# W2's conversion moves from the stage after the attention into the planned order of the attention

## The chip, the cores and the metric

The program runs on one core of a Trainium2 chip. The metric is the time of one execution on the device in microseconds (us). The engines have these names in the profile: PE is TensorE's matmuls and PEld its weight loads, DVE is VectorE, ACT is ScalarE, POOL is GpSimd and SP is SyncE, which here issues every transfer. Each engine works off its own list of instructions in order and waits where a semaphore tells it to.

## The reference

The input goes through a windowed attention (4 sequences of 576 positions, 8 heads of 64) and two blocks of dense layers. Weights that arrive as 64-bit floats are marked with a star.

```python
attn = softmax(mask(q @ k.T / 8))            # each position sees itself and the 63 before it
x    = (attn @ v) as [4, 576, 512]
h    = relu(x @ w_in)                         # w_in* [512, 1024]
u, v = halves of h;  v = layer_norm(v)
x    = (u * (w_spatial @ v + b)) @ w_out      # w_out* [512, 512]
u    = x + (relu(x.T @ w_tok1) @ w_tok2).T    # w_tok1*, w_tok2*
out  = u + relu(u @ w_ch1) @ w_ch2            # w_ch1* [512, 1536] (W1), w_ch2* [1536, 512] (W2)
```

## The kernel before

Every matrix product is done three times on fp32r operands: each operand is split into a high half (a cast on ACT) and a low half (value minus high half, a subtraction on DVE or POOL), and high x high, high x low and low x high are added up in one PSUM bank.

A weight that arrives as 64-bit words is first made into 32-bit floats. ACT scales the upper word (`down`, L136), DVE shifts the result left (L125) and joins three bits of the lower word to it (L131). In the following text these steps together are called decoding.

The two channel products use Strassen's scheme with seven products. For this, W1 and W2 are each cut into six blocks (j = 0 to 5). For each block of W2 four quarters are decoded, four sums of quarters are formed on POOL (L781), and the eight results are split and stored in the DRAM tile `scr` as pairs of halves, from where the second channel product loads them (`w<-scr`) 63 times.

**The attention stage** (up to about 208 us) is put in order by a planner in the program, the class `Steps`. Every piece of work is a step with an engine, a rank, an estimated time, the steps that it comes after, and buffers that it takes and gives back. The planner plays the stage through with these estimates: at each point it takes, on the engine that is free first, the ready step of the lowest rank, and writes its instructions there. What it writes is the order of each engine. In it the steps of a tile of attention are: scores S (PE), maxima M (DVE), exponentials X (ACT), norm N (DVE, L314 to L316), transposes T (PE, L485), copy C (ACT), product V (PE). Between them PE gets products of the first dense layer (`u`, `v`) and the spatial product (`s`) to fill its time.

**The stage after it** (about 240 to 360 us) holds the product with W_out (`W`, L830), transposes (`T`, L841), the token products (`A`, L849, with the relu `hh` on ACT at L855 and its low half `hl` on DVE at L856; `tok2`, L860) and then the first channel product (L927). Conversions of weights run beside these in slots: an object `bg` of the class `Line` is told after each product how much time it took, and for each 1.25 us it lets each open generator go one step on. A table names the slot at which each block of W1 and W2 begins: before, W2's blocks begin at slots 21, 33, 45, 56, 66 and 106, W1's at 27, 39, 51, 62, 71 and 90. All their instructions stand between those of the products on ACT, DVE and POOL. Names in the rows: `k` are decoded weights, `hl` from L775 and L776 the halves of W2 (another tile than `hl` from L856), `gh` and `gl` the halves of the gated input of W_out, `sh` and `sl` the halves of W1's sums.

**The last stage** (about 360 to 628 us) holds both channel products of three column groups.

## Time and profile before

| what | us |
|---|---|
| median of 3 runs (629.91 to 631.49) | 631.07 |
| the profiled execution | 629.98 |
| its span, first to last instruction | 628.2 |
| PE busy | 603.8 (96%) |
| PEld busy | 562.2 (89%) |
| DVE busy | 464.6 (74%) |
| ACT busy | 348.0 (55%) |
| POOL busy | 152.1 (24%) |

PE is the engine that has work all the time; the end of a matmul is modelled in this profile, so a stretch in which PE is called busy may hide small losses. To see where time can be won or lost, one looks for stretches in which PE is idle and for the instruction that ended the idle time.

### The profile page before, as it was taken

The numbers are of one execution on the slowest core, as the hardware profiler recorded it, in microseconds if no ns is written. First come the engines' busy times: TensorE is split into PE (matmuls) and PEld (weight loads), VectorE is DVE, ScalarE is ACT, GpSimd is POOL, SyncE is SP. The second block draws the span as 40 slices with busy tenths as digits, with TensorE's granted clock in tenths as the row PEclk, the third lists the DMA queues.
The fourth block names the chain that finished last, engine by engine and source line by source line (L and its number), as shares of the span: only waits on it lengthen the run. The fifth ranks groups of instructions, "written<-read, shape, count | busy, mean of one in ns | idle before, by whom it ended". The sixth has DMA issues, their size and how long they took to land.

```text
span 628.2 us, 11904 instructions
## 1 busy us (share of the span) xinstructions
PE 603.8 (96%) x4396; PEld 562.2 (89%) x4396; DVE 464.6 (74%) x980; ACT 348.0 (55%) x849; POOL 152.1 (24%) x169
## 2 busy tenths in 40 slices
PE   4999999999999999999889999999999999999997
PEld 2678899989998998788778898999999999999997
DVE  5999857754475545698878788898975889876882
ACT  5897756653484505686463555546643657444540
POOL 3000200100111000389778317140011140021320
PEclk8899999999999999999989999999999999999999
DMA  8956334440013503368876146674634575434652
GB/s 326 335 181 197 86 110 140 152 143 10 28 42 102 192 1 134 118 218 295 291 267 228 44 165 212 249 259 164 215 127 167 191 241 184 155 136 168 231 197 76
DMA packets 46354, 106.46 MB, mean 169 GB/s; under 512 B 4308, under 2 KB 16856, under 8 KB 46296
## 3 DMA queue, kind: packets, MB, share of 16 engines
q1 hardware_dynamic: 46296, 105.70, 48.8%
q8 instruction: 35, 0.57, 0.4%
q14 instruction: 23, 0.19, 0.1%
HBM read 86.81 MB, written 18.87 MB: 168 GB/s over the span
## 4 chain that ended last, share of the span: by engine, by line
PE 42%; DVE 5%; ACT 2%; issue 1%; ACTq 0%; DVEq 0%
PE A L1139 19%; PE mm L927 10%; PE A L927 8%; PE A L183 3%; DVE sl L171 1%; PE A L1223 1%; PE mm L183 1%; DVE hid L955 1%; DVE room L171 1%; ACT k L136 0%; DVE U L867 0%; DVE hid L921 0%; DVE k L131 0%; PE A L845 0%; ACT hid L952 0%
## 5 line engine op out<-in xcount | busy, mean ns | idle before, releaser
L1139 PE MATMUL A<-room,w 128*128 128x384 f32 x720 | 131.0, 335 | 0.7 <-DVE U L1175 0.7
L1139 PEld LDWEIGHTS A<-room,w 128*128 128x128 f32 x720 | 125.1, 188 | 2.1 <-DVE U L1175 1.0
L1133 ACT CAST room<-hid 128x384 fp32r<-128x384 f32 x120 | 61.3, 513 | 49.6 <-PE A L1139 38.4
L921 POOL TENSOR_TENSOR hid<-hid 128x384 f32<-128x384 f32 x36 | 43.8, 1226 | 181.9 <-DVE hid L921 150.5
L1134 DVE TENSOR_TENSOR room<-hid,room 128x384 fp32r<-128x384 f32 x120 | 73.2, 637 | 13.5 <-ACT room L1133 12.0
L183 PE MATMUL mm<-ws,room 128*128 128x288 f32 x416 | 60.9, 297 | 0.0
L183 PEld LDWEIGHTS mm<-ws,room 128*128 128x128 f32 x416 | 56.7, 188 | 0.5 <-DVE nm L297 0.3
L952 ACT ACTIVATE hid<-hid 128x384 f32<-128x384 f32 x54 | 28.0, 526 | 41.5 <-DVE hid L955 41.4
L776 POOL TENSOR_TENSOR hl<-k,hl 128x512 fp32r<-128x512 f32 (+1 forms) x24 | 31.2, 1305 | 73.8 <-ACT hl L775 72.1
L375 POOL TENSOR_SCALAR rstd<-mv 128x1 f32<-128x1 f32 x18 | 5.3, 296 | 178.8 <-DVE mv L373 165.2
L955 DVE TENSOR_TENSOR hid<-A,hid 128x384 f32<-128x384 f32 x54 | 29.5, 553 | 22.4 <-PE A L927 16.0
L306 ACT ACTIVATE pb<-pb,nm 128x128 f32<-128x128 f32 x96 | 37.2, 392 | 4.8 <-DVE nm L297 4.8
L927 PE MATMUL mm<-room,sh 128*128 128x384 f32 x144 | 37.2, 334 | 0.0
L406 DVE TENSOR_TENSOR U<-mm,U 128x288 f32<-128x288 f32 x32 | 14.6, 457 | 28.6 <-PE mm L183 28.3
L183 PE MATMUL mm<-xh,wi_h 128*128 128x384 f32 x96 | 33.4, 348 | 0.0
L183 PE MATMUL mm<-xh,wi_l 128*128 128x384 f32 x96 | 32.3, 336 | 0.0
L183 PE MATMUL mm<-xl,wi_h 128*128 128x384 f32 x96 | 32.2, 335 | 0.0
L183 PE MATMUL mm<-gh,wo_h 128*128 128x512 f32 (+1 forms) x80 | 30.5, 382 | 1.4 <-DVE U L867 0.9
L183 PE MATMUL mm<-gl,wo_h 128*128 128x512 f32 (+1 forms) x80 | 29.8, 372 | 1.3 <-DVE gl L827 1.3
L183 PE MATMUL mm<-gh,wo_l 128*128 128x512 f32 (+1 forms) x80 | 29.5, 369 | 0.0
L1164 DVE TENSOR_TENSOR U<-A,U 128x384 f32<-128x384 f32 x42 | 21.9, 551 | 10.3 <-PE A L1139 5.7
L485 PE MATMUL sp<-ident,pb 128*128 128x128 f32 x144 | 21.6, 284 | 5.6 <-DVE pb L316 2.1
(175 smaller groups left out, 1558.6 us busy)
## 6 DMA issues: line engine op xcount, KB each, us to landing
w<-scr SPq DMA_DIRECT2D x63, 512.0 KB, 4.1
k<-in_w_c SPq DMA_DIRECT2D x18, 512.0 KB, 4.7
scr<-hl SPq DMA_DIRECT2D x18, 512.0 KB, 5.3
k<-sums SPq DMA_DIRECT2D x18, 512.0 KB, 3.9
kk<-in_kT SPq DMA_DIRECT2D x16, 384.0 KB, 4.6
qq<-in_qT SPq DMA_DIRECT2D x18, 256.0 KB, 5.3
va<-in_v SPq DMA_DIRECT2D x18, 256.0 KB, 2.7
vb<-in_v SPq DMA_DIRECT2D x18, 256.0 KB, 3.6
```

The source lines that it names most:

```text
L183: nc.tensor.matmul(o, a, c, start=(i == 0), stop=(i == n - 1))
L306: nc.scalar.activation(out=pb[:, h, :], in_=scs[g][:, h - 4 * g, :] if mk is None else pb[:, h, :], func=AF.Exp, scale=SCALE if mk is None ...
L485: nc.tensor.transpose(pt[:, h, :], pb[:, 4 * g + h, :], ident)
L776: nc.gpsimd.tensor_tensor(out=hl[:, :, 1, :], in0=blk(s, n), in1=f(hl[:, :, 0, :]), op=ALU.subtract)
L921: eng.tensor_tensor(out=out, in0=a, in1=b, op=ALU.subtract)
L927: nc.tensor.matmul(o, a, m, start=first and i == 0, stop=i == len(todo) - 1, skip_group_check=True)
L952: nc.scalar.activation(out=o, in_=src, func=AF.Relu)
L955: nc.vector.tensor_tensor(out=o, in0=a, in1=b, op=ALU.add)
L1133: nc.scalar.copy(out=oh, in_=blk[j])
L1134: nc.vector.tensor_tensor(out=ol, in0=blk[j], in1=f(oh), op=ALU.subtract)
L1139: nc.tensor.matmul(acc[d], a, m, start=(first and j == 0 and i == 0), stop=(last and j == NJ - 1 and i == 2), skip_group_check=True)
L1164: nc.vector.tensor_tensor(out=at, in0=src, in1=at, op=ALU.add)
```

## The change

W2's conversion leaves the slots (`c2_steps` goes) and becomes steps of the planner (`c2_work`), with rank 6 + j, which is below everything that the attention needs. Words are fetched in pieces of 256 columns (256 KB) into two buffers `craw`; the decoded quarters lie in one buffer `cx` and the sums in one buffer `cy`, together 12 KB in each partition. Halves go through the attention's own three `raw` buffers and are stored one result at a time: 48 stores of 256 KB instead of 18 of 512 KB and 6 of 256 KB. The low halves, which POOL made (L776), are now made by DVE. W_out's decoding, which the planner held already, uses the same pieces and buffers and so comes in halves. Its 4 loads become 8. The gate behind which W_out's buffers open becomes a step of POOL. W1's blocks begin at slots 23, 30, 37, 62, 70 and 78.

```diff
-        S = Steps(sp=4, xo=1, mm=3, pb=PB, PT=2, v=2, qk=2, XT=2, vf=3, raw=3, wraw=3, wval=2)
+        S = Steps(sp=4, xo=1, mm=3, pb=PB, PT=2, v=2, qk=2, XT=2, vf=3, raw=3, wval=2, craw=2, cx=1, cy=1)
...
+        def fetch_words(name, src, after, rank, line):
+            def fetch():
+                raws[name] = stage.tile([P, 512], I32, tag="craw", name="craw", bufs=2)
+                nc.sync.dma_start(out=raws[name], in_=src.bitcast(I32))
+            S.add(("Lc", name), "SP", rank, 0, fetch, after=after, take=["craw"], hold=0.5, kb=256, line=line)
+        def scaled(name, x):
+            down(x, raws[name].rearrange("p (n w) -> p n w", w=2)[:, :, 1])
+        def joined(name, x):
+            y = x.bitcast(I32)
+            nc.vector.tensor_scalar(out=y, in0=y, scalar1=3, scalar2=None, op0=ALU.logical_shift_left)
+            nc.vector.scalar_tensor_tensor(out=y, in0=raws[name].rearrange("p (n w) -> p n w", w=2)[:, :, 0], scalar=29, in1=y, op0=ALU.logical_shift_right, op1=ALU.bitwise_or)
+        raws, halves = {}, {}
...
-            S.add(("Lo", k), "SP", 80, 0, fetch, after=["gate"], take=["wraw"], hold=0.5, kb=512, line="Lo")
-            S.add(("od", k), "ACT", 5, 0.7, first, after=[("Lo", k)], take=["wval"], hold=0.6)
-            S.add(("os", k), "DVE", 5, 0.45, part, after=[("od", k)])
-            S.add(("oo", k), "DVE", 5, 0.7, part, after=[("os", k)], give=["wraw"])
-            S.add(("oh", k), "ACT", 5, 0.6, high, after=[("oo", k)], hold=0.49)
+            for i in range(2):
+                n = ("o", k, i)
+                fetch_words(n, w_out[128 * k:128 * k + 128, 256 * i:256 * i + 256], ["gate"], 80, "Lo")
+                S.add(("cd", n), "ACT", 5, 0.4, lambda i=i: first(i), after=[("Lc", n)] + [("cd", ("o", k, 0))] * i, take=["wval"] * (not i), hold=0.33)
+                S.add(("cs", n), "DVE", 5, 0.7, lambda i=i, n=n: joined(n, g["x"][:, 256 * i:256 * i + 256]), after=[("cd", n)], give=["craw"], hold=0.65)
...
+        def c2_work(j):
+            rank = 6 + j
+            of = {}
+            def blk(s):
+                return of["xy"[s // 4]][:, 256 * (s % 4):256 * (s % 4) + 256]
+            def first(i):
+                if not i:
+                    of["x"] = stage.tile([P, 1024], F32, tag="cx", name="cx", bufs=1)
+                scaled((j, i), blk(i))
+            for i in range(4):
+                r, n = j + NJ * (i // 2), (j, i)
+                fetch_words(n, w_c2[128 * r:128 * r + 128, 256 * (i % 2):256 * (i % 2) + 256], [("ws", 5, 288)], 90, "Lc")
+                S.add(("cd", n), "ACT", rank, 0.4, lambda i=i: first(i), after=[("Lc", n)] + [("cd", (j, 0))] * (i > 0), take=["cx"] * (not i), hold=0.33)
+                S.add(("cs", n), "DVE", rank, 0.7, lambda i=i, n=n: joined(n, blk(i)), after=[("cd", n)], give=["craw"], hold=0.65)
+            def sums_():
+                of["y"] = stage.tile([P, 1024], F32, tag="cy", name="cy", bufs=1)
+                for o, a, b, op in ((4, 1, 3, ALU.add), (5, 4, 0, ALU.subtract), (6, 0, 1, ALU.subtract), (7, 2, 5, ALU.subtract)):
+                    nc.gpsimd.tensor_tensor(out=blk(o), in0=blk(a), in1=blk(b), op=op)
+            done = [("cs", (j, i)) for i in range(4)]
+            S.add(("sums", j), "POOL", rank, 2.6, sums_, after=done, take=["cy"])
+            def high(s):
+                halves[j, s] = stage.tile([P, 2 * WN], F32R, tag="raw", name="raw")
+                nc.scalar.copy(out=halves[j, s][:, :256], in_=blk(s))
+            def low(s):
+                nc.vector.tensor_tensor(out=halves[j, s][:, 256:], in0=blk(s), in1=f(halves[j, s][:, :256]), op=ALU.subtract)
+            def send(s):
+                nc.sync.dma_start(out=scr[s, j // 2, :, j % 2], in_=f(halves[j, s]).rearrange("p (h c) -> p h c", h=2))
+            for s in range(8):
+                S.add(("ch", j, s), "ACT", rank, 0.35, lambda s=s: high(s), after=[("cs", (j, s))] if s < 4 else [("sums", j)], take=["raw"], hold=0.27)
+                S.add(("cl", j, s), "DVE", rank, 0.4, lambda s=s: low(s), after=[("ch", j, s)] + [("sums", j)] * (s == 3), give=["cxcy"[s // 4 * 2:s // 4 * 2 + 2]] * (s % 4 == 3))
+                S.add(("Lh", j, s), "SP", 89, 0, lambda s=s: send(s), after=[("cl", j, s)], hold=0.5, kb=256, give=["raw"], line="Lh")
...
-        S.add("gate", None, 0, 0.0, gate, after=[("xl", last), ("xl", last - 1)])
+        S.add("gate", "POOL", 0, 0.0, gate, after=[("xl", last), ("xl", last - 1)])
         for k in range(4):
             wo_work(k)
+        for j in range(NJ):
+            c2_work(j)
...
-    def c2_steps(j):
-        x = yield from fetched([[w_c2[128 * r:128 * r + 128, :]] for r in (j, j + NJ)])
-        Y = [t.rearrange("p (s c) -> p s c", s=4) for t in (x, k4())]
-        def blk(s, n=1):
-            return Y[s // 4][:, s % 4:s % 4 + n, :]
-        def halves(s, n):
-            hl = k4(F32R, "hl").rearrange("p (s h c) -> p s h c", s=2, h=2)[:, :n]
-            nc.scalar.copy(out=hl[:, :, 0, :], in_=blk(s, n))
-            nc.gpsimd.tensor_tensor(out=hl[:, :, 1, :], in0=blk(s, n), in1=f(hl[:, :, 0, :]), op=ALU.subtract)
-            return lambda: nc.sync.dma_start(out=scr[s:s + n, j // 2, :, j % 2].rearrange("s p h c -> p s h c"), in_=f(hl))
-        send = [halves(0, 1), halves(2, 2)]
-        for o, a, b, op in ((4, 1, 3, ALU.add), (5, 4, 0, ALU.subtract), (6, 0, 1, ALU.subtract), (7, 2, 5, ALU.subtract)):
-            nc.gpsimd.tensor_tensor(out=blk(o), in0=blk(a), in1=blk(b), op=op)
-        yield from slots(5)
-        send.append(halves(4, 2))
-        send.pop(0)()
...
-        for at, w, j in ((21, 2, 0), (27, 1, 0), (33, 2, 1), (39, 1, 1), (45, 2, 2), (51, 1, 2), (56, 2, 3), (62, 1, 3), (66, 2, 4), (71, 1, 4), (90, 1, 5), (106, 2, 5)):
-            bg.add(at, c1_steps(j) if w == 1 else c2_steps(j))
+        for at, j in ((23, 0), (30, 1), (37, 2), (62, 3), (70, 4), (78, 5)):
+            bg.add(at, c1_steps(j))
```

What it moves on each engine is shown at three places. The first is DVE at the last two norms of the tiles 12 and 13, from 123 us on before; before:

```order
L378 TENSOR_SCALAR vf<-vf,mv,rstd 128x512
L314 TENSOR_SCALAR rs<-sm 128x4
L315 RECIPROCAL rs<-rs 128x4
L316 TENSOR_TENSOR pb<-pb,rs 128x512
L314 TENSOR_SCALAR rs<-sm 128x4
L315 RECIPROCAL rs<-rs 128x4
L316 TENSOR_TENSOR pb<-pb,rs 128x512
L384 TENSOR_TENSOR room<-vf,room 128x512
L406 TENSOR_TENSOR U<-mm,U 128x288
L540 TENSOR_TENSOR xl<-xo,xh 128x4x128
L406 TENSOR_TENSOR U<-mm,U 128x288
L540 TENSOR_TENSOR xl<-mm,xh 128x4x128
```

and now, from the same norm on (`raw<-cx,raw` and `raw<-cy,raw` are low halves of W2, `cx` its decoding):

```order
L314 TENSOR_SCALAR rs<-sm 128x4
L315 RECIPROCAL rs<-rs 128x4
L316 TENSOR_TENSOR pb<-pb,rs 128x512
L689 TENSOR_TENSOR raw<-cx,raw 128x256
L314 TENSOR_SCALAR rs<-sm 128x4
L315 RECIPROCAL rs<-rs 128x4
L316 TENSOR_TENSOR pb<-pb,rs 128x512
L384 TENSOR_TENSOR room<-vf,room 128x512
L689 TENSOR_TENSOR raw<-cx,raw 128x256
L689 TENSOR_TENSOR raw<-cy,raw 128x256 x2
L630 TENSOR_SCALAR cx<-cx 128x256
L631 SCALAR_TENSOR_TENSOR cx<-craw,cx 128x256
```

The norms keep their sequence, and splits and decoding of W2 stand between and behind them.

The second place is ACT up to the relu of the second token product of the second sequence, which the longest wait of PE hangs on; before:

```order
L836 COPY U<-mm 128x256
L855 ACTIVATE hh<-A 128x512
L775 CAST hl<-k_3866 128x2x256 x2
L136 ACTIVATE k_3993<-k_3877 128x512
L136 ACTIVATE k_3993<-k_3879 128x512
L753 CAST c1b<-k_3911 128x768
L348 CAST room<-A 128x512 x2
L855 ACTIVATE hh<-A 128x512
```

and now:

```order
L136 ACTIVATE k_4162<-k_4077 128x512
L348 CAST room<-A 128x512 x2
L864 COPY U<-mm 128x256
L883 ACTIVATE hh<-A 128x512
L808 CAST c1b<-k_4162 128x768
L348 CAST room<-A 128x512 x2
L883 ACTIVATE hh<-A 128x512
```

The two casts `hl` and the two scalings (L136) for W2 are gone from between the two relus `hh`.

The third place is DVE at the end of the token products, about 352 to 358 us before; before:

```order
L171 TENSOR_TENSOR room<-k_4193,room 128x768
L867 TENSOR_TENSOR U<-mm,U 128x288
L131 SCALAR_TENSOR_TENSOR k_4306<-k_4248,k_4306 128x512
L867 TENSOR_TENSOR U<-A,U 128x288
L171 TENSOR_TENSOR c1b<-k_4253,c1b 128x2x3x128
L867 TENSOR_TENSOR U<-mm,U 128x288
L131 SCALAR_TENSOR_TENSOR k_4306<-k_4250,k_4306 128x512
L867 TENSOR_TENSOR U<-A,U 128x288
L171 TENSOR_TENSOR room<-U,room 128x768
L867 TENSOR_TENSOR U<-mm,U 128x288
L867 TENSOR_TENSOR U<-A,U 128x288
L171 TENSOR_TENSOR sl<-k_4351,sh 128x1024
```

and now:

```order
L171 TENSOR_TENSOR room<-k_4417,room 128x768
L895 TENSOR_TENSOR U<-mm,U 128x288
L895 TENSOR_TENSOR U<-A,U 128x288
L171 TENSOR_TENSOR c1b<-k_4479,c1b 128x2x3x128
L895 TENSOR_TENSOR U<-mm,U 128x288
L895 TENSOR_TENSOR U<-A,U 128x288
L171 TENSOR_TENSOR room<-U,room 128x768
L895 TENSOR_TENSOR U<-mm,U 128x288
L895 TENSOR_TENSOR U<-A,U 128x288
L171 TENSOR_TENSOR sl<-k_4573,sh 128x1024
```

The two joins (L131) of W1's last block, which began at slot 90, stand earlier now.

## Rows read from the trace of the kernel before

**Rows 1.** Busy time by stretch: length; PE, PEld, DVE, ACT, POOL; PEclk, DMA share, GB/s.

```profile
72.00:208.00 136.00, 135.10 (x1362) 124.49 (x1359) 83.54 (x311) 78.68 (x258) 10.48 (x24) 1.00 0.29 94
208.00:240.00 32.00, 32.00 (x237) 31.68 (x236) 14.68 (x30) 6.83 (x12) 0.00 (x0) 1.00 0.27 93
240.00:400.00 160.00, 152.36 (x844) 135.51 (x843) 126.36 (x178) 91.94 (x167) 91.52 (x80) 0.99 0.60 207
320.00:340.00 20.00, 18.82 (x105) 16.95 (x106) 18.35 (x28) 10.87 (x19) 16.30 (x16) 0.91 0.55 207
```

**Rows 2.** Waits of TensorE, 240 to 400 us: us in total, times, longest.

```profile
PE mm L183 <- ACT hh L855: 1.8, 1, 1.8
PE A L927 <- DVE sl L171: 1.5, 3, 0.7
PE mm L183 <- DVE gl L827: 1.3, 3, 0.7
PE mm L183 <- DVE U L867: 1.2, 2, 0.9
PE mm L927 <- DVE U L867: 0.7, 1, 0.7
PE mm L183 <- ACT gh L826: 0.6, 1, 0.6
```

**Rows 3.** Timeline near 299 us: start, length, engine, line, operation.

```profile
298.61 2.71 POOL L776 TENSOR_TENSOR hl<-k,hl 128x512 fp32r<-128x512 f32 x2 [0.73 <-DMA sums<-k]
...
298.64 1.53 DVE L827 TENSOR_TENSOR gl<-U,gh 128x256 fp32r<-128x256 f32 x1
...
299.28 0.28 PE L183 MATMUL mm<-gh,wo_h 128*128 128x256 f32 x1
...
300.23 0.39 PE L183 MATMUL mm<-gl,wo_h 128*128 128x256 f32 x1 [0.67 <-DVE gl L827]
```

**Rows 4.** Timeline of ScalarE before the longest wait.

```profile
317.30 1.23 ACT L136 ACTIVATE k<-k 128x512 f32<-128x512 f32 x2
...
320.11 0.60 ACT L855 ACTIVATE hh<-A 128x512 fp32r<-128x512 f32 x1
```

**Rows 5.** Timeline of VectorE near 306 us.

```profile
305.38 1.11 DVE L131 SCALAR_TENSOR_TENSOR k<-k,k 128x512 int32<-128x512 int32 x1
```

**Rows 6.** Timeline of VectorE near 356 us.

```profile
355.34 0.68 DVE L131 SCALAR_TENSOR_TENSOR k<-k,k 128x512 int32<-128x512 int32 x1
...
357.59 0.45 DVE L867 TENSOR_TENSOR U<-mm,U 128x288 f32<-128x288 f32 x1
```

**Rows 7.** Timeline of VectorE: one `sl` split alone.

```profile
364.26 1.21 DVE L171 TENSOR_TENSOR sl<-k,sh 128x1024 fp32r<-128x1024 f32 x1
```

**Rows 8.** Timeline of VectorE near 388 us.

```profile
385.66 2.44 DVE L921 TENSOR_TENSOR hid<-hid 128x384 f32<-128x384 f32 x2
388.02 2.03 DVE L171 TENSOR_TENSOR sl<-k,sh 128x1024 fp32r<-128x1024 f32 x1
```

**Rows 9.** Groups by form, VectorE, 72 to 212 us: busy us, mean ns.

```profile
L131 DVE SCALAR_TENSOR_TENSOR val<-raw,val 128x512 int32<-128x512 int32 x4 | 2.7, 686 | 0.0
```

**Rows 10.** Groups by form, GpSimd, 255 to 400 us.

```profile
L776 POOL TENSOR_TENSOR hl<-k,hl 128x512 fp32r<-128x512 f32 x18 | 25.7, 1436 | 7.2 <-ACT hl L775 5.6 <-DMA sums<-k 0.7 <-DVE hid L955 0.7
...
L781 POOL TENSOR_TENSOR k<-k,k 128x256 f32<-128x256 f32 x12 | 13.0, 1082 | 0.4
L781 POOL TENSOR_TENSOR k<-k 128x256 f32<-128x256 f32 x12 | 10.4, 865 | 0.0
```

**Rows 11.** Groups by form, ScalarE, 255 to 400 us.

```profile
L775 ACT CAST hl<-k 128x256 fp32r<-128x256 f32 x6 | 2.4, 407 | 8.1 <-DVE k L131 8.1
```

**Rows 12.** Timeline of the attention near 123 us.

```profile
122.27 0.69 DVE L316 TENSOR_TENSOR pb<-pb,rs 128x512 f32<-128x512 f32 x1
...
124.22 0.27 PE L485 MATMUL sp<-ident,pb 128*128 128x128 f32 x1
```

**Rows 13.** Timeline of the attention near 128 us.

```profile
128.28 0.30 PE L485 MATMUL sp<-ident,pb 128*128 128x128 f32 x1 [0.90 <-DVE pb L316]
```

More of the change, by code (lines that the diff above doesn't have):

```diff
@@ L454, in tile_kernel @@
     opened = {}
+    HW, TW, NJ, CW = 384, 768, 6, 512
+    scr = tc.dram_tile([8, NJ // 2, P, 2, 2, 256], F32, name="scr")
+    sums = tc.dram_tile([NJ, P, 4, 256], F32, name="sums")
     wst_of = lambda tag, n, bufs: opened["wst"].tile([P, n], F32, tag=tag, name=tag, bufs=bufs)
@@ L612, in ws_load @@
             S.add(("ws", k, c), "DVE", 2.5, 0.45, part, after=[("wh", k, c)], give=["raw"], hold=0.38)
+        def fetch_words(name, src, after, rank, line):
[10 more added lines that the diff above has]
+        raws, halves = {}, {}
         def wo_work(k):
             g = {}
-            def fetch():
-                g["raw"] = wst_of("raw", 1024, 3).bitcast(I32)
-                nc.sync.dma_start(out=g["raw"], in_=w_out[128 * k:128 * k + 128, :].bitcast(I32))
-            def first():
-                r = g["raw"].rearrange("p (n w) -> p n w", w=2)
-                g["x"] = wst_of("val", 512, 2)
-                down(g["x"], r[:, :, 1])
-                g["it"] = to_f32(g["x"], [r[:, :, 0]])
-            def part():
-                next(g["it"])
+            def first(i):
+                if not i:
+                    g["x"] = opened["wst"].tile([P, 512], F32, tag="val", name="val", bufs=2)
+                scaled(("o", k, i), g["x"][:, 256 * i:256 * i + 256])
             def high():
@@ new lines, in wo_work, with first @@
+            S.add(("oh", k), "ACT", 5, 0.6, high, after=[("cs", ("o", k, i)) for i in range(2)], hold=0.49)
+            S.add(("ol", k), "DVE", 5, 0.7, low, after=[("oh", k)], give=["wval"])
+        def c2_work(j):
[3 more added lines that the diff above has]
+                return of["xy"[s // 4]][:, 256 * (s % 4):256 * (s % 4) + 256]
+            def first(i):
+                if not i:
+                    of["x"] = stage.tile([P, 1024], F32, tag="cx", name="cx", bufs=1)
[22 more added lines that the diff above has]
+                S.add(("Lh", j, s), "SP", 89, 0, lambda s=s: send(s), after=[("cl", j, s)], hold=0.5, kb=256, give=["raw"], line="Lh")
@@ L689, in tile_kernel @@
     psA = pool("psA", bufs=5, space=PSUM)
-    HW, TW, NJ, CW = 384, 768, 6, 512
-    scr = tc.dram_tile([8, NJ // 2, P, 2, 2, 256], F32, name="scr")
-    sums = tc.dram_tile([NJ, P, 4, 256], F32, name="sums")
     t1_h, t1_l, t2_h, t2_l, wo_h, wo_l = [opened[n] for n in ("t1_h", "t1_l", "t2_h", "t2_l", "wo_h", "wo_l")]
@@ L763, in c1_steps @@
         nc.sync.dma_start(out=sums[j], in_=y.rearrange("p (s c) -> p s c", s=4))
-    def c2_steps(j):
-        x = yield from fetched([[w_c2[128 * r:128 * r + 128, :]] for r in (j, j + NJ)])
-        Y = [t.rearrange("p (s c) -> p s c", s=4) for t in (x, k4())]
-        def blk(s, n=1):
-            return Y[s // 4][:, s % 4:s % 4 + n, :]
-        def halves(s, n):
-            hl = k4(F32R, "hl").rearrange("p (s h c) -> p s h c", s=2, h=2)[:, :n]
-            nc.scalar.copy(out=hl[:, :, 0, :], in_=blk(s, n))
-            nc.gpsimd.tensor_tensor(out=hl[:, :, 1, :], in0=blk(s, n), in1=f(hl[:, :, 0, :]), op=ALU.subtract)
-            return lambda: nc.sync.dma_start(out=scr[s:s + n, j // 2, :, j % 2].rearrange("s p h c -> p s h c"), in_=f(hl))
-        send = [halves(0, 1), halves(2, 2)]
-        for o, a, b, op in ((4, 1, 3, ALU.add), (5, 4, 0, ALU.subtract), (6, 0, 1, ALU.subtract), (7, 2, 5, ALU.subtract)):
-            nc.gpsimd.tensor_tensor(out=blk(o), in0=blk(a), in1=blk(b), op=op)
-        yield from slots(5)
-        send.append(halves(4, 2))
-        send.pop(0)()
-        send.pop(0)()
-        yield
-        send.append(halves(6, 2))
-        yield from slots(4)
-        send.pop(0)()
-        send.pop(0)()
     class Line:
```

## The prediction

> **What bounds the kernel now.** I read the busy times by stretch first. From 72 to 208 us PE is busy for 135.10 of 136.00 us, while DVE has 83.54 us of work, ACT 78.68 and POOL 10.48: the attention has free time on the three engines that convert weights, and PE sets its length. From 208 to 240 us PE is busy for all of 32.00 us. From 240 to 400 us PE has 152.36 of 160.00 us, so 7.64 us are idle, and there POOL carries 91.52 us of work and DVE 126.36 us [rows 1]. This is the stage whose slots hold the conversions. Next I read who ended PE's idle time in it: the groups shown add up to 7.1 us in 11 waits, and nearly all of them end with DVE or ACT finishing something that PE needs at once [rows 2]. Last I read the timeline at these waits, to see what stood ahead of the late instruction. The kernel is bound by PE, and the stage from 240 to 400 us by small waits behind conversions.
>
> **What goes.** Five places, each with the instruction of a conversion that made PE wait.
>
> *Near 299 us* the split `gl` of 256 columns takes 1.53 us, where an operation on two inputs of twice its width takes 0.69 us in the attention [rows 9]; it starts 0.03 us after POOL began two low halves of W2 that last 2.71 us, and PE waits 0.67 us for it [rows 3]. These rows also show what a wait costs beside its idle time. PE's matmul before the wait starts at 299.28 and the one after it at 300.23, that is 0.95 us apart, where matmuls of this form lie 0.12 us apart. The loss is 0.83 us, or 0.16 us more than the idle time. I add 0.16 us to each wait that goes.
>
> *Near 306 us* W2's join takes 1.11 us on DVE and ends at 306.49 [rows 5]. The two sums into U that free PSUM for PE stand right behind it; one of the waits for U (1.2 us in two) is this one, and the other, with the 0.7 us at the start of the channel product, lies near 356 us [rows 2].
>
> *Near 320 us* is the longest wait, 1.8 us for `hh` [rows 2]. ACT runs two scalings for W2 from 317.30 for 1.23 us, then a cast of W1 and two splits of transposes, and reaches `hh` at 320.11 [rows 4]. Without W2's scalings, and without the two casts of W2 ahead of them, W1's cast comes to stand earlier, and `hh` can start when its product ends. Part of this wait stays all the same: PE needs `hh` and then its low half soon after the product ends, and these take 0.60 us [rows 4] and about as much as the 0.69 us of [rows 9]. PE has some matmuls to fill a part of it. I leave 0.7 us. A second loss hangs on this wait. From 320 to 340 us the mean granted clock is 0.91, over the whole stage 0.99 [rows 1]: PE ran for a part of it at the lower of its two levels (1.2 in place of 2.4 GHz), after it had been idle. 20 us times 0.09 is 1.8 us, and by the other row 160 us times 0.01 is 1.6 us, so all of the stage's loss of clock lies here. I take 1.8 us.
>
> *Near 356 us* DVE joins a word of W1's last block (0.68 us at 355.34) among the sums into U; the sum that PE waits for starts at 357.59 [rows 6]. This block begins at slot 78 in place of 90, so both its joins, its shift and its split leave this place: three to four operations of the 0.68 us of the join or more, some 2 to 3 us of DVE, more than the 0.7 us and the shorter of the two waits for U that end here [rows 2].
>
> *Near 381 and 389 us* PE waits for the splits `sl` (1.5 us in three, one of them near 359) [rows 2]. One `sl` alone takes 1.21 us [rows 7]. At 388.02 it takes 2.03 us, behind two differences that took 2.44 us together [rows 8]. W2's last block is what POOL does there beside its own differences. POOL's differences `hid` stay, so some of the slow splits stay; the pair ahead of them gets faster by about 1 us, which is more than the waits (0.7 us at most).
>
> The waits for `gh` (0.6 us) and the rest of those for `gl` [rows 2] lie near 251 us, where W_tok2's conversion stays, and near 263 us, where W2's first block is decoded and no conversion stands between ACT's casts any more.
>
> The sum: 7.64 us idle, less 0.7 us that stays near 320, less 0.3 us that I leave near 251 us, gives 6.6 us. Eleven waits times 0.16 is 1.8 us. The clock is 1.8 us. Together 10.2 us go.
>
> **What comes.** The work itself does not shrink. POOL loses 25.7 us and the narrow rest of W2's low halves, and its 24 sums (13.0 + 10.4 us) move [rows 10]. In the attention they should cost less than the 0.87 to 1.08 us each of these rows; 24 times these means is 23 us at most, next to 10.48 us that POOL has there. DVE gets 24 decodings and 48 low halves of 256 columns. A join of 512 columns takes 0.69 us there [rows 9]; half of that up to the whole of it, for shift, join and split alike, gives 24 x (0.69 to 1.37) + 48 x (0.34 to 0.69), that is 33 to 66 us. I take 35, since a sum of 288 columns takes 0.45 us beside free engines [rows 6]. DVE then has 83.5 + 35 = 118 of 136 us. ACT gets 48 casts of 0.41 us and 24 scalings of about as much [rows 11], 29 us, and stands at 108 of 136 us. Both still fit, and what is left of W_out's decoding falls behind 208 us. There the spatial products keep PE busy for 32 us, while DVE has 14.68 us of work and ACT 6.83 [rows 1], so I cost it at nothing. Without this cover the first product with W_out would wait for its last half, up to the 2 us that one block's decoding takes.
>
> Whether PE waits depends on the slack in the chain M, X, N, T. A norm starts at 122.27 for 0.69 us, and its transposes start at 124.22, which is 1.26 us after its end [rows 12]. Once in the attention this slack is gone today, and PE waits 0.90 us for a norm [rows 13]. The order keeps the norms together and puts W2 between and behind them, and a step of W2 that has just begun holds a norm up by one split or one decoding, 0.4 to 0.7 us, less than the slack. The bound on the one side is the 0.9 us of today's one wait, should that go; on the other it is one lost hold of 0.7 us per norm, 20 norms from tile 8 on, 14 us. I take 2 us, twice the one wait that the trace has in these ten tiles.
>
> On SP the 24 fetches and 48 stores stand among the loads of `qq`, `kk`, `va` and `vb`. A store waits for its low half, and the loads behind it wait with it. These are issued a pair of tiles ahead, so I take nothing; what it could cost is within the 14 us. A cast waits for a free `raw`, hence for a store to land, and behind it on ACT stand exponentials and copies; that too is priced in the 14 us.
>
> One rule of the Trainium skill bears on the sums. *GPSIMD Engine Reference* (1. Specifications) says that GpSimd shares its SBUF interfaces with VectorE and that they contend where a VectorE instruction has two SBUF inputs. The trace agrees for `gl` and `sl` [rows 3, 7, 8]. *Trainium Architecture — The Big Picture* (What this means for kernel authors) calls it an exclusive lock and no sharing of bandwidth. By the lock, each of the 24 sums could hold an operation of DVE for its whole length, and the time would be the 637 us of the slower rival below. If the ports only shared their rate, the forecast's 2 us would stand.
>
> The forecast: the profiled execution took 629.98 us, its span of 628.2 and 1.8 us around it that nothing changes. 629.98 - 10.2 + 2.0 = 621.8 us for an execution like it, and it lies 1.1 us under the median of 631.07. So 622.9 us is the prediction, on the median's scale.
>
> **Rivals.**
>
> *W1 keeps the queues late.* W1's six blocks have decodings, splits and POOL sums of their own in the same stage and move closer together (slots 23, 30, 37). For it: near 320 us a cast of W1 stands ahead of `hh` too, and the waits near 356 us are W1's. Against it: between slots 50 and 62 hardly any conversion is left, and POOL's work there falls by more than half. If only the losses with W2's own instruction ahead of them go in part, half of 10.2 us, and 2 us come, the time is 631.07 - 5.1 + 2.0 = 628.0 us.
>
> *The sums hold up the norms* (slower). Place: DVE in the attention, when POOL's four sums of a block meet norms, low halves and joins, all with two SBUF inputs. Price: four sums at 0.87 to 1.08 us [rows 10] are 3.9 us; less the slack of 1.26 us, PE waits 2.6 us per block, six times, 16 us, and each wait of this length can be followed by a stretch at the lower clock as near 320 us, 1.8 us, 11 us in all. 631.07 - 10.2 + 16 + 11 = 648 us; without the clock 637 us. It decides from 10.2 us of new waits on, or 1.7 us per block. For it: DVE at 118 of 136 us has little to give back. Against it: the fourth quarter of a block is joined just ahead of the maxima, which read PSUM, so the sums run beside these and not beside norms.
>
> *Nothing is lost in the attention, and the one wait at 128 us goes as well.* Then 631.07 - 10.2 - 0.9 - the 1.0 us that I left = 619 us.
>
> **How the numbers follow.** The forecast (620.5 to 626) has 0.58, W1's rival 0.18, the case without loss 0.12, the slower rival 0.12; of the latter I put 0.03 within 0.3% of before (1.9 us, about what a measurement of this kernel can tell from no change), where it only just uses up the gain, and of W1's rival 0.05. So faster 0.83, same 0.08, slower 0.09. The range from 618 to 630 us leaves out the slower rival and little else.
>
> **What would show it.** In the profile after, PE idle from 240 to 400 us falls from 7.64 us to about 1, the granted clock from 320 to 340 us is 1.00, no wait for `gl` near 299 us and none for `sl` near 389 us is left, and POOL's work in the stage is 42 us or less (91.5 less the rows of W2 above). In the attention DVE stands near 118 of 136 us, and PE's waits there grow by 1 or 2 us. The prediction is wrong if PE waits for norms or for copies by more than 5 us in all between 72 and 208 us, if W1's steps keep `hh` late, or if SP's loads come late for the scores.

## The result, and the profile after

The changed kernel takes 622.15 us (median of 4 runs, 621.39 to 622.64) against 631.11 us of the kernel before beside it: a ratio of 0.986, 95% interval 0.9842 to 0.9878. Predicted were 622.9 us, 618 to 630. The profiled execution took 621.39 us, its span 619.5 us.

Both kernels do the same matmuls between four marks on PE (in the attention in an order that differs at 85 of 1307 places), so the span divides into stretches that can be compared: the start up to the first product with V of the tile that begins near 71 us (the 193rd matmul of L324); from there to the last product with V (the attention); from that to the first product with W_out (the rest of the spatial products); from that to the first product with W2's halves (the stage of the slots; L1139 before, L1167 after, the 3113th matmul); and the rest, up to the start of the last matmul.

| us, profiled executions | start | attention | behind it | stage of the slots | rest |
|---|---|---|---|---|---|
| before | 71.3 | 123.0 | 43.8 | 162.2 | 224.2 |
| changed | 71.0 | 124.4 | 45.9 | 150.3 | 224.3 |

11.9 us go in the stage that gave up W2's work; 1.4 us come in the attention and 2.1 us behind it. Nothing is given back later.

Busy time by stretch of the kernel after (columns as in [rows 1]):

```profile
72.00:208.00 136.00, 133.85 (x1344) 122.99 (x1341) 112.30 (x398) 98.34 (x324) 31.16 (x49) 1.00 0.63 216
208.00:240.00 32.00, 30.38 (x225) 29.91 (x224) 17.59 (x43) 9.69 (x21) 0.00 (x0) 1.00 0.46 153
240.00:400.00 160.00, 159.58 (x912) 145.60 (x911) 111.30 (x178) 79.61 (x143) 34.04 (x33) 1.00 0.33 111
320.00:340.00 20.00, 20.00 (x124) 18.13 (x123) 17.75 (x28) 8.66 (x14) 10.04 (x9) 1.00 0.08 31
```

From 240 to 400 us PE idles 0.42 us in place of 7.64, and the clock from 320 to 340 us is 1.00 in place of 0.91. POOL fell from 91.5 to 34.0 us there. The new idle time is in the two rows above: 2.15 us in the attention and 1.62 us behind it, where the kernel before had 0.90 and none [rows 1].

PE's waits after (us in total, times, longest), first from 72 to 208 us, then from 208 to 400 us; the second group answers to [rows 2]:

```profile
PE sp L488 <- DVE pb L316: 1.5, 2, 1.3
PE sp L488 <- DVE rs L314: 0.5, 1, 0.5
...
PE mm L183 <- DVE U L406: 1.5, 1, 1.5
PE mm L183 <- DVE gl L855: 0.2, 1, 0.2
PE mm L183 <- DVE hl L884: 0.2, 1, 0.2
```

Of the eleven waits of [rows 2] one of 0.2 us, for `gl`, is left; the other of 0.2 us, for `hl`, was 0.4 us before. The wait of 1.3 us for `pb` is the one of [rows 13], longer by 0.4 us. The wait of 1.5 us for `U` is new. Its timeline on PE, ACT and DVE (start, length; idle time before it and what ended that in brackets):

```profile
216.71 0.45 DVE L406 TENSOR_TENSOR U<-mm,U 128x288 f32<-128x288 f32 x1
...
220.43 0.29 PE L183 MATMUL mm<-ws,tails 128*128 128x288 f32 x1
220.56 0.43 ACT L136 ACTIVATE val<-craw 128x256 f32<-128x256 f32 x1 [4.58 <-DMA craw<-in_w_out]
221.02 0.29 DVE L630 TENSOR_SCALAR val<-val 128x256 int32<-128x256 int32 x1 [3.86 <-ACT val L136]
221.35 0.43 DVE L631 SCALAR_TENSOR_TENSOR val<-craw,val 128x256 int32<-128x256 int32 x1
221.69 0.45 DVE L406 TENSOR_TENSOR U<-mm,U 128x288 f32<-128x288 f32 x1
...
222.19 1.06 PE L183 MATMUL mm<-ws,room 128*128 128x288 f32 x6 [1.48 <-DVE U L406]
```

DVE works in order. It stood idle for 3.86 us in front of the shift and join of W_out's words, and the sum into U that gives PE its PSUM back stood behind them. ACT had waited 4.58 us for the words. SyncE's queue shows why they came late (times of issue):

```profile
210.13 0.33 SPq L621 DMA_DIRECT2D craw<-in_w_out  x1
210.56 0.97 SPq L692 DMA_DIRECT2D scr<-raw  x2
211.62 1.24 SPq L784 DMA_DIRECT2D k<-in_w_t  x2
213.64 0.34 SPq L621 DMA_DIRECT2D craw<-in_w_out  x1
214.03 0.48 SPq L784 DMA_DIRECT2D k<-in_w_t  x1
214.60 0.54 SPq L692 DMA_DIRECT2D scr<-raw  x1
215.39 0.33 SPq L621 DMA_DIRECT2D craw<-in_w_out  x1
```

Two loads of W_tok, 512 KB each, go out ahead of the fetch at 213.64 us, and a third, of 128 KB, ahead of the one at 215.39 us. The first of these two fetches landed 6.8 us after its issue; the profile has the landing of four of W_out's eight, and the other three took 2.6 to 3.1 us. Before the change W_out's last load went out at 203.1 us and W_tok's first at 208.6 us.

### The profile page after: what moved, and what is told of

Its sections match the earlier page's. It is cut to its first block, busy times and chain, and to the rows that moved or that the text cites. A ratio compares the mean times of both kernels' runs of the same rounds, so it can differ in the third digit from the quotient of the medians.

```text
span 619.5 us, 12149 instructions
## 1 busy us (share of the span) xinstructions
PE 600.2 (97%) x4396; PEld 560.6 (90%) x4396; DVE 472.6 (76%) x1066; ACT 352.7 (57%) x889; POOL 114.7 (19%) x145
## 4 chain that ended last, share of the span: by engine, by line
PE 62%; DVE 4%; DMA 4%; ACT 2%; issue 1%; POOL 0%; ACTq 0%
PE A L1167 19%; PE mm L183 13%; PE mm L955 12%; PE A L955 9%; PE A L183 6%; DMA scr<-raw 3%; PE A L873 1%; DMA craw<-in_w_out 1%; PE A L1251 1%; DVE pb L297 1%; DVE raw L689 0%; ACT raw L686 0%; DVE pb L316 0%; DVE st L372 0%; DVE hid L949 0%
## 5 line engine op out<-in xcount | busy, mean ns | idle before, releaser
L1167 PE MATMUL A<-room,w 128*128 128x384 f32 x720 | 131.1, 335 | 0.7 <-DVE U L1203 0.7
L1167 PEld LDWEIGHTS A<-room,w 128*128 128x128 f32 x720 | 125.1, 188 | 2.1 <-DVE U L1203 1.0
L1162 DVE TENSOR_TENSOR room<-hid,room 128x384 fp32r<-128x384 f32 x120 | 71.9, 625 | 13.9 <-ACT room L1161 12.2
L949 POOL TENSOR_TENSOR hid<-hid 128x384 f32<-128x384 f32 x36 | 44.2, 1239 | 202.8 <-DVE hid L949 160.0
L813 POOL TENSOR_TENSOR k<-k 128x256 f32<-128x256 f32 x12 | 9.7, 832 | 107.1 <-ACT gh L854 59.4
L855 DVE TENSOR_TENSOR gl<-U,gh 128x512 fp32r<-128x512 f32 (+1 forms) x20 | 13.3, 667 | 21.1 <-ACT gh L854 21.0
L170 ACT CAST sh<-k 128x1024 fp32r<-128x1024 f32 x18 | 18.9, 1050 | 15.7 <-PE mm L955 5.9
```

The lines of the kernel that those rows point to most:

```text
L170: nc.scalar.copy(out=hi, in_=x)
L949: eng.tensor_tensor(out=out, in0=a, in1=b, op=ALU.subtract)
L1162: nc.vector.tensor_tensor(out=ol, in0=blk[j], in1=f(oh), op=ALU.subtract)
L1167: nc.tensor.matmul(acc[d], a, m, start=(first and j == 0 and i == 0), stop=(last and j == NJ - 1 and i == 2), skip_group_check=True)
```

## The experiments

All runs, with the same stretches (us, from the profiled execution of each; the ratio is to the kernel before on the same chip):

| run | median | ratio, 95% interval | start | attention | behind it | slots | rest |
|---|---|---|---|---|---|---|---|
| changed, again (e9) | 621.10 | 0.9853, 0.9829–0.9878 | 72.3 | 123.7 | 45.8 | 150.4 | 224.2 |
| e1 join behind the sum | 619.80 | 0.9844, 0.9824–0.9864 | 70.8 | 124.1 | 44.6 | 150.3 | 224.3 |
| e2 W2's tail behind W_out | 622.19 | 0.9875, 0.9852–0.9897 | 73.9 | 124.4 | 45.8 | 150.4 | 224.3 |
| e3 W1 in its old slots | 624.30 | 0.9907, 0.9890–0.9924 | 72.8 | 124.1 | 45.8 | 152.9 | 224.2 |
| e4 transfers only | 618.31 | 0.9817, 0.9800–0.9835 | 71.1 | 123.0 | 44.2 | 150.3 | 224.3 |
| e5 two joins later | 621.35 | 0.9866, 0.9841–0.9891 | 70.9 | 123.8 | 46.1 | 150.3 | 224.2 |
| e6 casts on POOL | 623.95 | 0.9911, 0.9881–0.9941 | 71.6 | 125.1 | 48.2 | 150.3 | 224.3 |
| e7 sums three times | 648.00 | 1.0285, 1.0259–1.0312 | 71.1 | 145.4 | 51.3 | 150.3 | 224.2 |
| e8 low halves on POOL | 627.24 | 0.9952, 0.9932–0.9973 | 70.9 | 125.9 | 49.3 | 150.3 | 224.2 |
| e10 W_tok behind W_out | 619.62 | 0.9832, 0.9811–0.9854 | 70.8 | 123.9 | 44.1 | 150.3 | 224.3 |
| e11 e1 and e10 | 620.54 | 0.9832, 0.9807–0.9857 | 72.9 | 123.9 | 43.8 | 150.3 | 224.3 |
| e12 sums on DVE | 624.01 | 0.9897, 0.9876–0.9919 | 73.0 | 122.1 | 50.0 | 150.3 | 224.2 |

The start, which no edit touches, takes 70.8 to 73.9 us in these executions. So a median can't tell 1 us. The stretches can, since two executions of the changed kernel agree to 0.1 us in each but the start and the attention (0.7 us).

**The wait behind the attention.** e1 moves two instructions on DVE:

```diff
-                S.add(("cs", n), "DVE", 5, 0.7, ..., after=[("cd", n)], give=["craw"], hold=0.65)
+                S.add(("cs", n), "DVE", 5, 0.7, ..., after=[("cd", n)] + [("G", 2, 1, 288)] * (k == 3), give=["craw"], hold=0.65)
```

> Edit: of W_out's last 128 rows, the two joins of words on DVE are put behind the fourth sum into U (L406) of the last spatial product that the planner orders, and nothing else; the same instructions, the same transfers. Theory: the 1.5 us for which PE waits at 220.4 us for U L406, and the 0.5 us at 224, come from DVE standing in those joins for words that land only at 220.5 and 222.8 us, while the sums that free PSUM are queued behind. Then the wait at 220 us goes, the first product with W_out comes at about 239.5 instead of 241.3 us, and the time is about 620.4 us (619.9 to 621.0). Rival: the words come late because the DMA queues are full there, and PE waits for another thing soon after (the splits of W_out, or the next sums); then the time stays at 622 +- 0.4 us.

The wait at 220 us went and 1.3 us with it (45.9 to 44.6 us). The words came no earlier (ACT at 220.3 us), so DVE's order did turn a late word into a wait. A wait of 0.6 us, for a join in front of these, showed at 216 us. e5 moved that one too (the same edit, for the second join of the third block, behind an earlier sum):

> Edit: as e1, and the second join of W_out's third block also comes behind the second sum into U of the planner's last spatial product. In e1 PE still waited 0.58 us at 216.3 us, because that join stood on DVE for words that came at 215.5 us, ahead of the sum for U. Theory: this wait goes too, the first product with W_out comes at about 239.0 us, and the time is 0.4 to 0.7 us under e1's: 619.1 to 619.5 us. Rival: the buffer that this join frees later delays the last fetch of W_out, and PE waits as much at 222 us: 619.8 to 620.5 us.

```profile
PE mm L183 <- DVE U L406: 2.1, 1, 2.1
```

That is PE's one wait from 208 to 240 us in e5. It is as long as the rival had it, but it did not come in the rival's way: the last two fetches went out at 212.7 and 216.3 us, no later than in e1 (213.2 and 216.4 us). What changed is ACT's order, in which the cast of W_out's third block now stands behind the scaling of the fourth block's first words:

```profile
219.99 0.43 ACT L136 ACTIVATE val<-craw 128x256 f32<-128x256 f32 x1 [5.29 <-DMA craw<-in_w_out]
220.32 0.60 ACT L644 CAST wo_h<-val 128x512 fp32r<-128x512 f32 x1
```

DVE stood idle for 4.41 us in front of the split that needs this cast, again with a sum behind it. Moving joins moves the wait; it doesn't bring the words. The median, 621.35 us, lies over both ranges. e2 and e10 ask what makes the words late:

```diff
-                fetch_words(n, w_c2[...], [("ws", 5, 288)], 90, "Lc")
+                fetch_words(n, w_c2[...], [("ws", 5, 288)] if j < 5 else [("cs", ("o", 3, 1))], 90, "Lc" if j < 5 else "Lc5")
```

> Edit: W2's last row group (its fetches, words, sums, halves and stores) is held back until W_out's words are all joined; so W_out's fetches no longer share the two buffers and SP's queue with W2's stores. Theory that the transfers of W2's tail delay W_out: W_out's last words land before 217 us, the wait at 220 us goes, and the first product with W_out comes at about 239.5 us; W2's last group then runs between 212 and 235 us, where DVE works 17.6 of 32 us and ACT 9.7; time about 620.4 us (619.8 to 621.2). Rival: the six W_tok loads, not W2's stores, keep the last two fetches: the wait stays, and the group adds its own on top; 622 to 624 us.

Neither came out whole. The wait at 220 us went: without W2's last group W_out's last fetch goes out 17.3 us after the last product with V, where it was 20.0 us. It still takes 5.5 us to land, behind W_tok's loads. And PE waited 0.8 and 0.7 us at 231 and 239 us, for sums behind W2's last group and behind the split `gl`, which waits for `gh`; for that ACT waited until W2's last stores had landed:

```profile
235.26 0.41 ACT L686 CAST raw<-cy 128x256 fp32r<-128x256 f32 x1 [0.49 <-DMA scr<-raw]
238.42 1.14 ACT L854 CAST gh<-U 128x512 fp32r<-128x512 f32 x2 [2.75 <-DMA scr<-raw]
```

So W2 must not come behind W_out here. e10 leaves W2 where it is, and puts W_tok's loads behind W_out's words:

```diff
+                    opened["last"] = g["x"]
...
+        early += [k4() for _ in range(3)]
+        for t in early:
+            nc.vector.tensor_copy(out=t[:, :1], in_=opened["last"][:, 511:512])
...
-            raw = k4().bitcast(I32)
+            raw = (early.pop(0) if early else k4()).bitcast(I32)
```

> The changed kernel itself once more, on the same chip as the next three, so that differences of 1 us can be read: 621 to 623 us, with the wait of 1.5 us at 220 us.

> Edit: the first three loads of W_tok (1.5 MB) wait for W_out's last join on DVE (a copy of one column into each of their buffers, three copies of 128x1 on DVE); nothing else changes. In the changed kernel two of these loads go out at 211.6 us and a third at 214.0 us, ahead of W_out's last two fetches, which then take 6.8 and 7.4 us to land. Theory: these loads make the last words late; behind W_out they leave its fetches 3 to 4 us each, the last words are joined by 218 us, and of the 1.6 us that PE idles at 220 and 224 us at least 1 us goes: 1 to 1.8 us under the changed kernel. W_tok, 6 us later, is still in time for the transposes after 258 us. Rival: W2's stores and the two buffers make the words late; then the wait stays, and the time is that of the changed kernel within 0.5 us, or longer if W_tok comes late.

```profile
212.96 0.33 SPq L621 DMA_DIRECT2D craw<-in_w_out  x1
213.61 0.32 SPq L693 DMA_DIRECT2D scr<-raw  x1
214.56 0.33 SPq L621 DMA_DIRECT2D craw<-in_w_out  x1
214.93 0.46 SPq L693 DMA_DIRECT2D scr<-raw  x1
220.19 0.90 SPq L787 DMA_DIRECT2D k<-in_w_t  x2
```

In e9 the wait is 1.8 us, at 221 us. The three buffers of W_tok take four loads, 1.25 MB in all and not 1.5. W2's stores and the two buffers are still there; only W_tok went back. The last two of W_out's fetches now land after 2.7 and 3.9 us (6.8 us for the first of them before), the last shift starts at 218.9 us, and the view of waits lists none for PE from 208 to 240 us. 1.7 us of the 2.1 are back (45.8 to 44.1 us), and the median is 1.5 us under e9's; by the ratios' intervals alone the two would not be told apart. The last sum behind a join still comes a little late, at 220.1 us, where PE's matmuls start 0.36 us apart in place of 0.13, so e11 adds e1's order:

> Edit: e1 and e10 together: W_out's last joins stand behind the sum into U, and the first W_tok loads wait for them. Theory: both remove the same wait, so together they give hardly more than the better one: the first product with W_out at 238.6 to 239.4 us, the time 1.6 to 2.6 us under the changed kernel. Rival: with W_tok behind joins that are themselves moved later, its words come late for ACT, whose scalings of W_tok then hold up the splits that the products with W_out wait for: within 1 us of the changed kernel, or slower.

Behind the attention it takes 43.8 us, as before the change. W_tok's loads in front of W_out's last fetches and DVE's order made this loss together: without the first 0.3 us of it is left (e10), without the second 0.8 us (e1), without both nothing. W2's last group has a share too, since it delays the last fetch (e2). In the stretch behind the attention e10 and e11 are 1.7 and 2.0 us faster than e9. By the medians e11 is 0.6 us faster than e9 and not the 1.6 us at least that were expected; in the profiled execution its start took 2.1 us longer than e10's.

**The attention.** e4 leaves all arithmetic of W2 out, the sums and both halves too, and a store waits for a fetch alone:

```diff
-                S.add(("cd", n), "ACT", rank, 0.4, ...)
-                S.add(("cs", n), "DVE", rank, 0.7, ...)
...
+                S.add(("cs", n), None, 6 + j, 0, lambda: None, after=[("Lc", n)], give=["craw"])
+                for s in (i, i + 4):
+                    S.add(("Lh", j, s), "SP", 89, 0, lambda s=s: send(s), after=[("cs", n)], hold=0.5, kb=256, line="Lh")
```

> Edit: W2's fetches and its 48 stores stay in the planner's order, but all arithmetic of its conversion (ACT, DVE and POOL) is left out: every store sends the same constant tile, and a fetch's buffer is free as soon as it has landed. Nothing of W2 is computed. Theory: the 3.2 us by which the first product with W_out is later than before the change come from the work on DVE and ACT (1.1 us in the attention, 2 us behind it); without it that product comes at 238 to 239 us, and the time is 619 to 620 us. Rival: the transfers (4.6 MB more in the attention, the loads of v and q landing later) cost it; then at least 1 us of the attention's loss stays, and the time is 621 to 622 us.

```profile
72.00:208.00 136.00, 135.10 (x1356) 124.50 (x1352) 82.64 (x311) 77.13 (x257) 10.54 (x24) 1.00 0.67 227
```

The DMA engines carry 227 GB/s here where the kernel before had 94 [rows 1], and PE's busy time is the same 135.10 us; the attention takes 123.0 us in both. So the traffic costs nothing: 133 GB/s more for 136 us are 18 MB (the 4.6 MB of the expectation are too few). The loss comes with the arithmetic. Whether it is its instructions or the order that the planner writes because of them, e4 doesn't tell, since in it PE's matmuls in the attention stand in the order of before. The median, 618.31 us, is 0.7 us under the theory's range. e6, e8 and e12 move a part of the arithmetic to another engine, each on one engine's line of the planner, with its estimated time (`"ACT"` to `"POOL"` and `nc.scalar.copy` to `nc.gpsimd.tensor_copy` for the casts; `"DVE"` to `"POOL"` for the low halves; `"POOL"` to `"DVE"` for the sums).

> Edit: as e5, and the 48 casts of W2's high halves (256 columns each) move from ACT to POOL. Theory: the 1.1 to 1.4 us lost in the attention are ACT's, since W2's casts (two of them, 0.71 us, at 144.9 us) run between the two copies of P transposed that give PE its PSUM back; without them on ACT PE's waits at 126.7 and 145 us fall by 0.8 us in all, and the time is 0.5 to 1 us under e5's. Rival: POOL, now with some 40 us more, is late for the norms' rstd, and the products wait for them, or its work slows DVE's operations: 1 us or more over e5's.

> Edit: as e5, and the 48 low halves (128x256) are subtracted on POOL in place of DVE. That takes some 20 us from DVE's 112 and adds some 45 us to POOL in the attention. Theory: DVE isn't what PE waits for there but for the sums behind W_out's words; so within 0.5 us of e5's, a little under it if the wait at 126.7 us (1.3 us for pb) shrinks. Rival: POOL and DVE hinder each other, DVE's operations with two SBUF operands take longer, and the norms come late: 1 to 4 us over e5's.

PE's waits from 120 to 150 us in e6, and from 120 to 130 us in e8:

```profile
PE sp L488 <- DVE pb L316: 1.9, 1, 1.9
```

```profile
PE sp L488 <- DVE pb L316: 0.9, 1, 0.9
...
```

In e6 the wait near 145 us is gone and the one near 128 us is 1.9 us; in e8 the latter is back at the 0.9 us of before, but two others come at 143 and 145 us (1.1 and 0.8 us). This points to two low halves on DVE in front of a norm (at 123 us) as what adds 0.4 us to the wait at 128 us, and to the casts on ACT for the one at 145 us. It does not show it, since the planner's order moves a little with each edit. What makes the wait of 1.9 us in e6 can be read on DVE and POOL:

```profile
125.66 2.70 DVE L689 TENSOR_TENSOR raw<-cx,raw 128x256 fp32r<-128x256 f32 x3
128.29 0.16 DVE L314 TENSOR_SCALAR rs<-sm 128x4 f32<-128x4 f32 x1
```

```profile
126.30 0.92 POOL L679 TENSOR_TENSOR cy<-cx 128x256 f32<-128x256 f32 x1
```

Three low halves beside the sums take 2.70 us, ahead of the norm that PE needs; alone one takes 0.42 us. The mean granted clock from 120 to 140 us is 0.91; of the 1.4 us that this attention takes over e5's the waits account for 0.3, so the clock costs about 1 us, an estimate. Each edit loses more than it saves: the attention takes 125.1 and 125.9 us, and behind it PE waits 2.4 us for U in e6, where W2's last group comes behind W_out as in e2, and 3.6 us in e8, where W_out's words come late and ACT has the order of e5. Both theories on the total fell: e6 is 2.6 us over e5, as its rival had it, and e8 5.9 us, more than its rival's 4. POOL is the wrong place for this work.

> Edit: the changed kernel with W2's 24 sums on DVE in place of POOL, at the same rank in the planner; POOL keeps the norms alone, DVE gets some 10 us more in the attention. Three times the sums cost 26 us, since rstd then stood behind batches of nearly 10 us. Theory: a batch of 3.3 us is still short enough, so one share of the sums costs nothing now; on DVE they come to stand ahead of pb and the sums for U, and the time is 0 to 1.5 us over the changed kernel. Rival: POOL's batches already cost part of what is lost in the attention; then 0.5 to 1 us under it.

PE waits nowhere in the attention, which takes 122.1 us, 1.6 us less than in e9: in this stretch the rival's gain, and more. Yet the planner, which counts the sums on DVE, also put the same matmuls there in another order (at 435 of 1307 places), and W2's last fetches behind W_out's, to 223 us; so what the sums alone cost on POOL isn't settled. That tail costs 4.2 us in two waits for U, one of them as in e2, and the mean granted clock is 0.91 from 240 to 260 us. In all the time is 2.9 us over e9's, so neither range held.

**How near the slower rival was.** e7 repeats the sums in place:

```diff
-                for o, a, b, op in ((4, 1, 3, ALU.add), ..., (7, 2, 5, ALU.subtract)):
+                for o, a, b, op in ((4, 1, 3, ALU.add), ..., (7, 2, 5, ALU.subtract)) * 3:
```

> Edit: as e5, and POOL does each of W2's four sums three times over (72 in place of 24; the order on the engines stays). About 40 us more of POOL's work, in batches of some 10 us in place of 3.4. Theory: the sums are far from the norms that PE needs and from the halves that are due, so the time stays within 0.5 us of e5's. Rival (the slower case of the prediction): the batches hold up rstd on POOL and so the norms and the products with W_s and the next scores, and they slow DVE's operations with two operands in SBUF; then 2 us or more over e5's, with waits of PE for tiles of the norms between 72 and 208 us.

27 us come (over e5), 21.6 of them in the attention. My theory fell; POOL, DVE, ACT and PE near 182 us:

```profile
172.14 0.91 POOL L679 TENSOR_TENSOR cy<-cx 128x256 f32<-128x256 f32 x1
...
181.07 0.73 POOL L679 TENSOR_TENSOR cy<-cx,cy 128x256 f32<-128x256 f32 x1
181.88 0.22 POOL L375 TENSOR_SCALAR rstd<-mv 128x1 f32<-128x1 f32 x1
182.19 0.57 POOL L376 TENSOR_TENSOR rstd<-rstd,mhalf 128x1 f32<-128x1 f32 x1
```

```profile
182.79 0.55 DVE L378 TENSOR_SCALAR vf<-vf,mv,rstd 128x512 f32<-128x512 f32 x1 [5.87 <-POOL rstd L376]
```

```profile
183.37 0.62 ACT L382 CAST room<-vf 128x512 fp32r<-128x512 f32 x1 [8.25 <-DVE vf L378]
183.90 0.55 ACT L344 ACTIVATE U<-mm 128x128 f32<-128x128 f32 x2
```

```profile
184.50 0.80 PE L183 MATMUL mm<-wi_h,xh 128*128 128x512 f32 x1 [2.93 <-ACT U L344]
```

Twelve sums hold POOL for 9.7 us. `rstd` stands behind them, DVE's normalization and all that DVE has behind it wait 5.87 us for it, ACT 8.25 us, and PE 2.93 us for the PSUM that ACT frees. With four sums the batches are 2.9 to 3.4 us. A second loss is the clock (e7, columns as in [rows 1]):

```profile
72.00:216.00 144.00, 129.46 (x1268) 117.00 (x1266) 103.07 (x371) 88.69 (x303) 54.48 (x78) 0.94 0.55 184
```

PE idles 14.5 us, and its mean granted clock is 0.94, where the changed kernel has 1.00 from 72 to 208 us; 144 us times 0.06 is 8.6 us, an estimate of what the clock takes of the 21.6. The prediction's slower rival had another place, DVE, where sums meet its operations; a queue on POOL in front of `rstd` stands in e7's own expectation only. The length at which a batch begins to cost lies somewhere between 3.4 and 9.7 us.

**W1's slots.**

```diff
-        for at, j in ((23, 0), (30, 1), (37, 2), (62, 3), (70, 4), (78, 5)):
+        for at, j in ((27, 0), (39, 1), (51, 2), (62, 3), (71, 4), (90, 5)):
```

> Edit: W1's six conversions return to the slots that they had before the change (27, 39, 51, 62, 71, 90); W2 stays in the attention. Theory of the prediction: W2's own work made nearly all the waits of PE between 240 and 400 us; of W1 only its last block, near 356 us, had a share (the waits of 0.75 and 0.34 us for U there). So 0.5 to 1.6 us come back, near 355 us: 622.7 to 623.8 us, and the waits for gl near 299, hh near 319 and sl near 389 us stay away. Rival: the other slots of W1 made a good part of the gain, and the waits for gl or hh return: over 625 us.

PE's waits from 240 to 400 us:

```profile
PE mm L955 <- DVE U L895: 0.8, 1, 0.8
PE mm L183 <- DVE U L895: 0.3, 1, 0.3
PE A L955 <- DVE sl L171: 0.3, 1, 0.3
PE mm L183 <- DVE gl L855: 0.2, 1, 0.2
PE mm L183 <- DVE hl L884: 0.2, 1, 0.2
```

The stage takes 152.9 in place of 150.3 us. The first three waits came back at 352 to 357 us, where W1's last block has its joins on DVE among the sums; the last two are those that the changed kernel has too, and the waits near 299, 320 and 389 us stayed away. 2.5 of the 11.9 us were W1's slots, 9.4 us W2's absence. The theory had the place and the waits; it had the loss at 1.6 us at most.

## Why the prediction was right, point by point

*What goes: 10.2 us predicted, 11.9 measured.* Both kernels do the same 853 matmuls of this stage in the same order, so their starts can be compared one by one. Idle time: 6.6 us predicted, 7.64 - 0.42 = 7.2 us measured; near 320 us 0.2 us are left where I had left 0.7. The late start behind each wait: 11 x 0.16 = 1.8 us predicted, 1.9 us measured. The clock: 1.8 us predicted, 1.3 us measured, since from 322.1 to 324.7 us twelve matmuls start mostly 0.24 us apart in place of 0.13:

```profile
322.36 0.44 PE L183 MATMUL A<-t_l,hh 128*128 128x288 f32 x1
322.60 0.44 PE L183 MATMUL A<-t_h,hl 128*128 128x288 f32 x1
```

The other 1.5 us the prediction had at nothing. About 1 us of them is the second matmul behind a wait, which starts 0.1 us late as well; near 299 us it comes at 300.45, 0.22 us after the first [rows 3], and the same two lie 0.12 us apart after the change:

```profile
300.45 0.28 PE L183 MATMUL mm<-gh,wo_l 128*128 128x256 f32 x1
```

Most of the rest are waits too short for the view of waits. The places were right: none of the waits near 299, 306, 356 and 381 to 389 us is left, and e3 shows the one near 356 us to be W1's, as the prediction had it.

*What comes in the attention: 2.0 us predicted, 0.6 and 1.4 us measured in two executions.* DVE has 112 us (118 predicted), ACT 98 (108), POOL 31 (10.5 + 23 at most). The loads of `v` and `q` behind W2's stores were costed at nothing; e4 shows it for the traffic, and PE waits for no load in the attention after the change.

*W_out behind 208 us: nothing predicted, 2.1 us measured.* This is the step that failed: "There the spatial products keep PE busy for 32 us, while DVE has 14.68 us of work and ACT 6.83 [rows 1], so I cost it at nothing." Free time on an engine is no cover when the engine stands idle at an instruction whose data is late, with what PE needs behind it. DVE was idle for 14.4 of the 32 us, and PE waited for it. The prediction named up to 2 us, but for W_out's first product, and it followed SP's queue only among the attention's loads, not past W_tok's (e10, e11).

*The two errors cancel.* 1.7 us more go than predicted (11.9 less 10.2), and 1.5 us more come (3.5 less 2.0). That the time lies within 0.8 us of the prediction is luck to this extent.

*Rivals.* W1 keeps no queue late to speak of: in its new slots 0.42 us of idle time is left in the stage, in the old ones it lost 2.5 us. The case without loss (619 us) did not come, since both the attention and W_out's tail lost time; e10 comes near it, but only because more went than predicted. The slower rival's price went by the sums' meeting DVE's operations. The Trainium skill speaks of an exclusive lock between GpSimd and VectorE (*Trainium Architecture — The Big Picture*, What this means for kernel authors). Where the two meet, the trace shows a long hold: of W2's low halves in the changed kernel those of `cx`, which can run beside the sums, take up to 0.96 us, in place of 0.42. But they seldom meet where it matters. Of the 20 norms there only one runs beside work on POOL, and all take 0.69 us; with three times the sums four of 19 run beside them and take 0.90 to 1.09 us. So the prediction's reason against this rival, that the sums do not run beside norms, held, and most of e7's loss is POOL's order, in which `rstd` waits, and the clock. The low halves and the norms in the attention after, then the norms in e7 (72 to 208 us; busy us, mean ns):

```profile
L689 DVE TENSOR_TENSOR raw<-cx,raw 128x256 fp32r<-128x256 f32 x23 | 11.6, 527 | 0.0
L689 DVE TENSOR_TENSOR raw<-cy,raw 128x256 fp32r<-128x256 f32 x20 | 8.1, 419 | 1.5 <-ACT raw L686 1.3
L316 DVE TENSOR_TENSOR pb<-pb,rs 128x512 f32<-128x512 f32 x20 | 13.8, 692 | 0.7
```

```profile
L316 DVE TENSOR_TENSOR pb<-pb,rs 128x512 f32<-128x512 f32 x19 | 14.4, 758 | 0.7
```

What stays open: which part of the 0.6 to 1.4 us in the attention is the sums' on POOL, and which the planner's order.

## What to carry to other kernels

Work moved under a bound engine is free only if its data is there when its turn comes: on an in-order engine a late word holds up everything behind it, however idle the engine looks. So follow the moved step's loads through the DMA queue, past the loads of the next stage too, and order the queue by when words are due. On an engine that serves a chain of small steps, look at the length of one uninterrupted batch: in e7 POOL had 54 of 144 us of work and still held up the chain, by batches of 9.7 us. And a wait costs more than its idle time, here up to 0.26 us in the two matmuls behind it.
